# One broadcast transfer per block of x for both array halves, in a fused attention and bilinear-GLU kernel

## Chip, cores and metric

The kernel runs on one core of one Trainium2 chip. The metric is the device time of one launch in microseconds (us); the time before is the median of three runs.

## What is computed

x has 2048 tokens of width 576; attention has 32 heads of 18, and the GLU an inner width of 4608. Everything is float32.

```python
xn = layernorm(x)                                        # [1, 2048, 576], no scale or bias
q, k, v = heads(xn @ wqkv)                               # 32 heads of 18
s = concat(softmax(q @ k.T * 18 ** -0.5) @ v) @ wo
g = silu(((xn @ w_gate) * (xn @ w_up)) @ w_down)         # inner width 4608
out = x + s * g
```

## The kernel before

Float32 operands are split into a high and a low part, and each product is made of three matmuls (high by high, low by high, high by low), which is why x, the weights and the softmax inputs exist twice.

The kernel has a short first stage (layer norm, transposes of x into columns, the projections to q, k and v), one long main loop, and a short end (the projection with wo, silu, sum). In the main loop three kinds of work are interleaved on TensorE:

- scores: `a_item` (L651) makes scores for the row maxima, `b_item` (L703) makes them again for the exponentials;
- `pv_group` (L714): a visit, in which all of TensorE multiplies probabilities by v, 64 matmuls, about 7 us, twice per head;
- the GLU: `gu_op` (L756) for gate and up, `down_op` (L807) for the down projection.

Scores and GLU use 64 of the 128 rows of the array, so two streams run side by side on the two array halves. Half 0 (partitions 0 to 63) does the up products, half 1 (partitions 64 to 127) the gate products. Each half reads its own copy of x, from its own partitions.

The GLU goes over four chunks of 512 tokens (`NCH`); within a chunk over 18 units (`NF2`) of two column tiles each. The columns of x for the current chunk stand in the two tiles `xg` (`xc` in the profile), each 128 partitions x 9 slots x 512. They hold nine blocks of 64 input columns, each with a high and a low part; block b lies in slots 2b and 2b + 1, counted over both tiles, so that block 4 is cut between them. A tile of gate or up is 27 matmuls, three for each block in order (`TERMS`). There is one buffer for x: in the last tile of a chunk, each block of the next chunk is loaded over the one just used, from the copy `sx` in DRAM. That happens three times, at the three passages from one chunk to the next; the first chunk is loaded by `x_first` (L535).

Before the change each half brings its own copy as soon as it has itself used the blocks: half 0 by the queue of SyncE (SP), half 1 by that of GpSimd (Pool). Blocks 0 and 1, 2 and 3, 5 and 6, 7 and 8 come in pairs (L468), block 4 in two parts (L465), each to 64 partitions. On SP stand also the loads of weights (`wgu`, `wd`), of the q and k stacks (`whole`, `turning`, 18 rows each, L319) and of raw weights. Every queue is served in program order.

The order of the instructions is written out ahead by a planner (`order`). It keeps a clock for each half (`clk`), times at which the engines come free (`free`, `engine`) and one for the DMA queue (`moved`), takes the next instruction of the half that lags, and lets it go if `can_go` says that its inputs are due. For x that is `there["x", chunk, block, half]`, asked for the first tile of a new chunk only. TensorE then runs this order as it stands and waits on semaphores where a due time was too early.

```python
def moved(start, size):                                          # L1024
    queue[0] = max(queue[0], start) + size / 0.24
    return queue[0] + 2.0
...
if c and q == 0 and n % 2 == 0:                                  # L1216, in can_go
    return there.get(("x", c, k // 3, r), 1e9) <= now
```

When the gate tile is done, VectorE multiplies it with up (L769), ScalarE rounds the product to its high part (L774), and Pool makes the low part (L787).

Of the kernel before, what the change touches and what calls it, by code (L numbers as in the profile page):

```python
# [20 lines left out]
FT = mybir.dt.float32  # L21
# [20 lines left out]
def kernel(  # L42
# [10 lines left out]
    nc = tc.nc  # L53
# [20 lines left out]
    sx = dram.tile([NCH, 9, 64, 2, 512], FT, name="sx")  # L74
# [93 lines left out]
    clk, free, split_at = [0.0, 0.0], {"DVE": 0.0, "ACT": 0.0, "POOL": 0.0}, {}  # L168
# [7 lines left out]
    def engine(eng, start, length):  # L176
        start = max(free[eng], start)
        free[eng] = start + max(length - HIDDEN[eng], 0.03)
        return start + length
# [278 lines left out]
    def x_part(b, part):  # L458
        return divmod(2 * b + part, 9)

    def x_block(c, b, r):
        queue = nc.gpsimd if r else nc.sync
        if b == 4:
            for part in range(2):
                queue.dma_start(xg[part][r:r + 64, 8 - 8 * part, :].bitcast(FT), sx[c, b, :, part, :])  # L465
        elif b in (1, 3, 6, 8):
            i, k = x_part(b - 1, 0)
            queue.dma_start(xg[i][r:r + 64, k:k + 4, :].rearrange("p (b e) s -> p b e s", b=2).bitcast(FT),  # L468
                            sx[c, b - 1:b + 1].rearrange("b p e s -> p b e s"))

    vbox, vrows, vturn = {}, [], [0]

# [125 lines left out]
    for t in range(8, NT):  # L598
# [4 lines left out]
        if t == 11:  # L603
            xg = [xcp.tile([128, 9, 512], FR, name="xc")]
# [28 lines left out]
    with ExitStack() as mid:  # L633
# [115 lines left out]
        def gu_start(r, n):  # L749
            ready(gdone, n)  # L750
            return bank("g", 1, slots[r, "g"])

        def gu_op(r, n, ps, k):
            a, b, part = TERMS[k]
            i, e = x_part(b, part)
            nc.tensor.matmul(ps, gw[n][half[r], a, :], xg[i][half[r], e, :], start=k == 0,  # L756
                             stop=k == len(TERMS) - 1)
# [39 lines left out]
        def alone(u, n):  # L797
            return u == len(units) - 1 and n == 7

        def down_start(r, u):  # L800
            ready(ddone, u)
            return bank("g", 1, slots[r, "d"])

        def down_op(r, u, s, i, ps, n, by):
            own = alone(u, 2 * s + i)
            j, a, e = DTERMS[n]
            op = nc.tensor.matmul(ps[:, 0:HALF], hs[u][half[r], j, a, s * 128:(s + 1) * 128],  # L807
                             dw[u][half[r], j, e, i * HALF:(i + 1) * HALF],
                             start=(own or r == 0) and n == 0, stop=(own or r == 1) and n == len(DTERMS) - 1)
            if not own and r == 0 and n == len(DTERMS) - 1:  # L810
                handing[u, s, i] = by.nop()
                after(handing[u, s, i], op)
            if not own and r == 1 and n == 0:
                after(op, handing.pop((u, s, i)))
# [9 lines left out]
        def by_act(u, i, at):  # L824

            if units[u][1] == 0:
                return i == 1
            if u == len(units) - 1 or len(sums_later) == 2 or len(st_end) > 1 and st_end[-2 + len(sums_later)] > at:
                return False
            return max(free["ACT"], at) < max(free["DVE"], at)  # L830
# [18 lines left out]
        def down_end(u, s, i, ps, act):  # L849
            c, q = units[u]  # L850
            cs = slice(i * HALF, (i + 1) * HALF)
            if q == 0 and c >= 2:
                ready(sdone, 4 * c - 8 + s)
            a = sums(4 * c + s)[:, cs]
            if s == 3:
                seen[u] = seen.get(u, 0) + 1
                if seen[u] == 2:
                    d_get(u + 1)
            if act:
                if q == 0:  # L860
                    nc.scalar.activation(a, ps[:, 0:HALF], AF.Copy)
                else:
                    st = mp.tile([128, HALF], FT, name="st", bufs=2)
                    nc.scalar.activation(st, ps[:, 0:HALF], AF.Copy)  # L864
                    sums_later.append((a, st, u, s))
                    return
            elif q == 0:
                nc.vector.tensor_copy(a, ps[:, 0:HALF])
            else:
                nc.vector.tensor_tensor(a, a, ps[:, 0:HALF], op=OP.add)  # L870
            down_summed(u, s)
# [69 lines left out]
        def wo_fetch():  # L941
            wos[0] = xcp.tile([128, 8, D], FR, name="wos", tag="xc")
            for k in (0, 4):
                nc.sync.dma_start(wos[0][:, k:k + 4, :].bitcast(FT), swo[:, k:k + 4, :])
# [2 lines left out]
            wos[1] = wpool.tile([128, 2, D], FR, name="wos2", tag="wgu", bufs=2)  # L947
            nc.sync.dma_start(wos[1].bitcast(FT), swo[:, 8:10, :])

        passed, xdone = {}, []  # L950

        def stream(r, kind):

            def glu(n):
                c, q = units[n // 2]
                box = []
                for k in range(len(TERMS)):
                    def work(k=k):
                        if k == 0:
                            box.append(gu_start(r, n))  # L960
                        gu_op(r, n, box[0], k)
                        if q == NF2 - 1 and n % 2 and k % 3 == 2 and c < NCH - 1:
                            b = k // 3
                            x_block(c + 1, b, 64 * r)
                            if b in (1, 3, 4, 6, 8):
                                if r:
                                    at = engine("POOL", clk[r] + 0.5, 0.75 + 0.6 * (b == 4)) + 3.0
                                else:
                                    at = moved(clk[r] + 0.5, 0.285 if b == 4 else 0.57)
                                for e in (b,) if b == 4 else (b - 1, b):  # L970
                                    there["x", c + 1, e, r] = at
                        if n == 2 * len(units) - 1 and k == 13:
                            xdone.append(r)
                            if len(xdone) == 2:
                                wo_fetch()
                        if k == len(TERMS) - 1:
                            highs.append((gate_end if r else up_end)(n, box[0]))
                    end = (("DVE", 0.685) if r else ("ACT", 0.595)) if k == len(TERMS) - 1 else None
                    yield 0.231, k == 0, work, end, ("g", n, k), len(TERMS)

            def down(u, n):
                own = alone(u, n)
                key = u, n, r * own
                s, i = divmod(n, 2)
                for k in range(len(DTERMS)):
                    def work(k=k):
                        if (own or r == 0) and k == 0:
                            passed[key] = down_start(r, u)
                        down_op(r, u, s, i, passed[key], k, {"POOL": nc.gpsimd, "ACT": nc.scalar, "DVE": nc.vector}[soonest()])
                        if (own or r) and k == len(DTERMS) - 1:  # L990
                            acts.append(by_act(u, i, clk[r] + 0.33))
                            down_end(u, s, i, passed.pop(key), acts[-1])
                    end = None
                    if (own or r) and k == len(DTERMS) - 1:
                        end = (None, 0.0)
                    yield 0.132, (own or r == 0) and k == 0, work, end, ("d", u, 6 * n + k), len(DTERMS)

            if kind == "g":
                for n in range(2 * len(units)):
                    yield from glu(n)  # L1000
            else:
                for u in range(len(units)):
                    for n in range(8):
                        yield from down(u, n)
# [19 lines left out]
# [5 lines that stand above are left out]
        due, jobs, rows_done = [], [], {}  # L1029
        there, queue = {}, [0.0]  # L1030
        na = nb = 0
        part_work = len(units) * (2 * 27 * 0.231 + 4 * 12 * 0.132)
        part = part_work + (TOTAL + N + LEAD) * 0.231
# [199 lines left out]
        def soonest():  # L1233
            at = {eng: max(free[eng], clk[0] + 0.35 + (0.0 if eng == "POOL" else 0.2)) for eng in free}
            return min(at, key=at.get)
# [215 lines left out]
```

## Time and profile before

| | |
|---|---|
| median of three runs | 2621.14 us (2620.93 to 2621.47) |
| profiled execution, whole | 2619.56 us |
| its span, first to last instruction | 2617.8 us |
| TensorE, weight load, VectorE, ScalarE, GpSimd busy | 99%, 82%, 68%, 60%, 26% |
| mean granted TensorE clock | 0.998 |
| DMA: moved, mean rate | 434.33 MB, 166 GB/s |

Times are in us from the start of the span. Busy shares are of the span. In rows of the timeline stand the start, the duration, the engine (PE is TensorE, DVE VectorE, ACT ScalarE; SPq is SyncE's queue), the line, the operation, output and input tiles and count, and in brackets the idle time just before with what ended it. Rows of waits have the waiting instruction, what it waited for, then us in total, times, and the longest. Rows of windows give the stretch, the length, the busy time and count of TensorE, weight load, VectorE, ScalarE and GpSimd, the granted clock, the share of the 16 DMA engines that was busy (1 is all of them) and GB/s. Rows of DMA issues have the engine, the count, KB each, and for Pool the median us from issue to landing. A row with a spread of three numbers gives minimum, median and maximum in ns.

### The profile page before, as it was taken

The numbers are of one execution on the slowest core, as the hardware profiler recorded it, in microseconds if no ns is written. First come the engines' busy times: TensorE is split into PE (matmuls) and PEld (weight loads), VectorE is DVE, ScalarE is ACT, GpSimd is POOL, SyncE is SP. The second block draws the span as 40 slices with busy tenths as digits, with TensorE's granted clock in tenths as the row PEclk, the third lists the DMA queues.
The fourth block names the chain that finished last, engine by engine and source line by source line (L and its number), as shares of the span: only waits on it lengthen the run. The fifth ranks groups of instructions, "written<-read, shape, count | busy, mean of one in ns | idle before, by whom it ended". The sixth has DMA issues, their size and how long they took to land.

```text
span 2617.8 us, 59481 instructions
## 1 busy us (share of the span) xinstructions
PE 2595.7 (99%) x24504; PEld 2144.6 (82%) x24504; DVE 1782.2 (68%) x2951; ACT 1559.3 (60%) x3121; POOL 687.6 (26%) x721
## 2 busy tenths in 40 slices
PE   8999999999999999999999999999999999999999
PEld 7899878877778778878778887788888788877799
DVE  7208776767767777777767777677777777777136
ACT  4224666677766556666556666566666666666712
POOL 3114434444431212222121212222221222211015
PEclk9999999999999999999999999999999999999999
DMA  7799767676764445454564443453454443533366
GB/s 238 244 295 257 205 179 193 184 188 182 188 166 138 143 140 160 145 161 153 155 169 120 137 137 123 155 161 131 140 162 130 141 138 132 151 123 123 117 219 212
DMA packets 206544, 434.33 MB, mean 166 GB/s; under 512 B 82592, under 2 KB 132416, under 8 KB 176064
## 3 DMA queue, kind: packets, MB, share of 16 engines
q1 hardware_dynamic: 202096, 415.48, 52.5%
q0 software_dynamic: 4176, 15.04, 1.8%
q8 instruction: 193, 3.16, 0.5%
q14 instruction: 79, 0.65, 0.1%
HBM read 314.64 MB, written 110.56 MB: 162 GB/s over the span
## 4 chain that ended last, share of the span: by engine, by line
PE 96%; DMA 2%; SPq 1%; DVE 1%; issue 0%; ACT 0%; DVEq 0%
PE pg L756 35%; PE pg L714 17%; PE pg L807 16%; PE pa L651 11%; PE pb L703 9%; PE pg L1403 2%; PE pb L445 2%; PE pa L445 2%; PE pg L503 1%; DMA xc<-sx 1%; SPq L535 1%; DVE mx L653 0%; PE pb L1380 0%; DMA sv<-vo 0%; PE pa L703 0%; PE pg L385 0%
## 5 line engine op out<-in xcount | busy, mean ns | idle before, releaser
L653 DVE TENSOR_REDUCE mx<-pa 128x1 f32<-128x512 f32 x2016 | 1348.5, 687 | 379.1 <-PE pa L651 172.9
L705 ACT ACTIVATE pt<-pb 128x512 f32<-128x512 f32 x2003 | 1153.3, 603 | 501.1 <-PE pb L703 379.2
L756 PE MATMUL pg<-xc,wgu 64*128 64x512 f32 x7776 | 1401.9, 392 | 9.3 <-DMA xc<-sx 9.2
L756 PEld LDWEIGHTS pg<-xc,wgu 64*128 64x128 f32 x7776 | 1061.9, 186 | 55.6 <-DMA xc<-sx 6.4
L807 PE MATMUL pg<-wd,hs 64*128 64x288 f32 x6816 | 829.4, 293 | 0.0
L807 PEld LDWEIGHTS pg<-wd,hs 64*128 64x128 f32 x6816 | 775.9, 185 | 11.6 <-issue 1.7
L651 PE MATMUL pa<-whole,turning 54*128 54x512 f32 x1999 | 782.5, 398 | 0.8 <-DVE mx L653 0.7
L703 PE MATMUL pb<-whole,turning 56*128 56x512 f32 x1986 | 778.5, 398 | 0.0
L714 PE MATMUL pg<-pt,vt 128*32 128x512 f32 x4096 | 454.0, 595 | 0.0
L787 POOL TENSOR_TENSOR hs<-us,hs 128x512 fp32r<-128x512 f32 x144 | 185.9, 1291 | 1005.0 <-ACT hs L774 757.7
L651 PEld LDWEIGHTS pa<-whole,turning 54*128 54x128 f32 x1999 | 363.7, 184 | 71.5 <-issue 50.5
L703 PEld LDWEIGHTS pb<-whole,turning 56*128 56x128 f32 x1986 | 361.6, 184 | 7.7 <-ACT pt L705 0.6
L714 PEld LDWEIGHTS pg<-pt,vt 128*32 128x32 f32 x4096 | 126.6, 110 | 285.8 <-issue 281.5
L834 POOL TENSOR_TENSOR acc<-acc,st 128x288 f32<-128x288 f32 x290 | 233.3, 808 | 465.5 <-ACT st L864 297.1
L720 DVE TENSOR_TENSOR oc<-oc,pg 128x512 f32<-128x512 f32 x32 | 22.0, 688 | 220.5 <-PE pg L714 220.5
L254 POOL TENSOR_TENSOR wgu<-wraw,wgu 128x384 fp32r<-128x384 f32 x108 | 108.1, 1018 | 211.4 <-ACT wgu L253 120.0
L718 ACT ACTIVATE oc<-pg 128x512 f32<-128x512 f32 x32 | 19.1, 598 | 231.6 <-PE pg L714 231.6
L870 DVE TENSOR_TENSOR acc<-acc,pg 128x288 f32<-128x288 f32 x255 | 114.2, 449 | 41.4 <-PE pg L807 39.2
L769 DVE TENSOR_TENSOR us<-pg,us 128x512 f32<-128x512 f32 x144 | 98.5, 684 | 50.6 <-PE pg L756 31.6
L762 ACT ACTIVATE us<-pg 128x512 f32<-128x512 f32 x144 | 86.6, 602 | 69.2 <-PE pg L756 65.4
L864 ACT ACTIVATE st<-pg 128x288 f32<-128x288 f32 x290 | 119.9, 414 | 12.1 <-PE pg L807 6.0
L774 ACT ACTIVATE hs<-us 128x512 fp32r<-128x512 f32 x144 | 91.2, 634 | 26.1 <-DVE us L769 26.1
(147 smaller groups left out, 1288.7 us busy)
## 6 DMA issues: line engine op xcount, KB each, us to landing
wgu<-swg SPq DMA_DIRECT2D x102, 1152.0 KB
wd<-swd SPq DMA_DIRECT2D x50, 1152.0 KB
swg<-wgu SPq DMA_DIRECT2D x36, 1152.0 KB
whole<-sqk SPq DMA_DIRECT2D x192, 144.0 KB
turning<-sqk SPq DMA_DIRECT2D x384, 72.0 KB
swd<-wd SPq DMA_DIRECT2D x18, 1152.0 KB
sqk<-hl SPq DMA_DIRECT2D x32, 512.0 KB
wraw<-in_B_w_up_dram SPq DMA_DIRECT2D x36, 288.0 KB
```

The source lines that it names most:

```text
L254: nc.gpsimd.tensor_tensor(w[:, 9 + b:12 + b, :], raw[:, b:b + 3, :], w[:, b:b + 3, :].bitcast(FT), op=OP.subtract)
L651: nc.tensor.matmul(p, q[rows, t * 128:(t + 1) * 128], k[rows, c * 512:(c + 1) * 512], start=True, stop=True)
L653: nc.vector.tensor_reduce(mx[h][:, t, c:c + 1], p, axis=AX.X, op=OP.max)
L703: nc.tensor.matmul(p, k[rows, t * 128:(t + 1) * 128], q[rows, c * 512:(c + 1) * 512], start=True, stop=True)
L705: nc.scalar.activation(pt[t, c // 2][:, c % 2, :], p, AF.Exp, scale=scale)
L714: nc.tensor.matmul(p[32 * c:32 * c + 32, :], vt[h // 2][:, t, 6 * (h % 2):6 * (h % 2) + 32], pt[t, c // 2][:, c % 2, :], start=t == ts[0], ...
L756: nc.tensor.matmul(ps, gw[n][half[r], a, :], xg[i][half[r], e, :], start=k == 0, stop=k == len(TERMS) - 1)
L787: nc.gpsimd.tensor_tensor(hj[:, 1, :], h32, hj[:, 0, :].bitcast(FT), op=OP.subtract)
L807: op = nc.tensor.matmul(ps[:, 0:HALF], hs[u][half[r], j, a, s * 128:(s + 1) * 128], dw[u][half[r], j, e, i * HALF:(i + 1) * HALF], start=( ...
L834: nc.gpsimd.tensor_tensor(a, a, st, op=OP.add)
L864: nc.scalar.activation(st, ps[:, 0:HALF], AF.Copy)
L870: nc.vector.tensor_tensor(a, a, ps[:, 0:HALF], op=OP.add)
```

## The change

Each block comes by itself, in one transfer over all 128 partitions: the source is read twice, by a leading dimension of two with step 0. It is issued once both halves have used the block, by SP for even blocks and by Pool for odd ones; block 4 goes in two parts, one for each tile. In the planner each block counts 0.45 MB on the DMA queue, an odd one also 0.75 us on Pool and 2 us more, and both halves get the same due time.

```diff
-    def x_block(c, b, r):
-        queue = nc.gpsimd if r else nc.sync
+    def both_halves(tile, src):
+        return tile.bitcast(FT), src.unsqueeze(0).broadcast_to([2] + list(src.shape))
+
+    def x_block(c, b):
+        queue = nc.gpsimd if b % 2 else nc.sync
         if b == 4:
             for part in range(2):
-                queue.dma_start(xg[part][r:r + 64, 8 - 8 * part, :].bitcast(FT), sx[c, b, :, part, :])
-        elif b in (1, 3, 6, 8):
-            i, k = x_part(b - 1, 0)
-            queue.dma_start(xg[i][r:r + 64, k:k + 4, :].rearrange("p (b e) s -> p b e s", b=2).bitcast(FT),
-                            sx[c, b - 1:b + 1].rearrange("b p e s -> p b e s"))
+                queue.dma_start(*both_halves(xg[part][:, 8 - 8 * part, :], sx[c, b, :, part, :]))
+        else:
+            i, k = x_part(b, 0)
+            queue.dma_start(*both_halves(xg[i][:, k:k + 2, :], sx[c, b]))
...
-        passed, xdone = {}, []
+        passed, xdone, xhalf = {}, [], set()
...
                             b = k // 3
-                            x_block(c + 1, b, 64 * r)
-                            if b in (1, 3, 4, 6, 8):
-                                if r:
-                                    at = engine("POOL", clk[r] + 0.5, 0.75 + 0.6 * (b == 4)) + 3.0
-                                else:
-                                    at = moved(clk[r] + 0.5, 0.285 if b == 4 else 0.57)
-                                for e in (b,) if b == 4 else (b - 1, b):
-                                    there["x", c + 1, e, r] = at
+                            if (c, b) in xhalf:
+                                x_block(c + 1, b)
+                                at = moved(clk[r] + 0.5, 0.45)
+                                if b % 2:
+                                    at = max(at, engine("POOL", clk[r] + 0.5, 0.75) + 2.0)
+                                there["x", c + 1, b, 0] = there["x", c + 1, b, 1] = at
+                            xhalf.add((c, b))
```

## The prediction

> **What bounds the kernel now.** I read the page first (engines, slices, chain), then the table of waits, then the timeline around the three places where the change acts, then the DMA share in short windows.
>
> ```profile
> span 2617.8 us, 59481 instructions
> PE 2595.7 (99%) x24504; PEld 2144.6 (82%) x24504; DVE 1782.2 (68%) x2951; ACT 1559.3 (60%) x3121; POOL 687.6 (26%) x721
> PE 96%; DMA 2%; SPq 1%; DVE 1%; issue 0%; ACT 0%; DVEq 0%
> PE pg L756 <- DMA xc<-sx: 9.2, 3, 4.0
> PEld pg L756 <- DMA xc<-sx: 6.4, 2, 3.3
> ```
>
> TensorE is busy for 99% of the span and carries 96% of the chain. The kernel is bound by the order of its matmuls, and whatever makes TensorE stand still is paid in full. The loads of x touched here (xc<-sx) are the one DMA on which a main-loop matmul waits for long: 9.2 us in three waits. (The 6.4 us of PEld lie over the same stretches, so they are not added.) The waits stand in the timeline of TensorE:
>
> ```profile
> 754.01 1.05 PE L756 MATMUL pg<-xc,wgu 64*128 64x512 f32 x5 [3.96 <-DMA xc<-sx]
> 1360.73 0.50 PE L756 MATMUL pg<-xc,wgu 64*128 64x512 f32 x2 [2.89 <-DMA xc<-sx]
> 1365.66 0.79 PE L756 MATMUL pg<-xc,wgu 64*128 64x512 f32 x2 [2.37 <-DMA xc<-sx]
> ```
>
> They fall at the first two of the three passages from one chunk of 512 tokens to the next. The third passage has none. So what can be won is 9.2 us, 0.35% of the span. What can be lost depends on how long the new loads take.
>
> **What moves.** The issues of x, from the list of DMA issues, and the loads that stand near them in SP's queue:
>
> ```profile
> xc<-sx SPq DMA_DIRECT2D x12, 512.0 KB
> xc<-sx POOLq DMA_DIRECT2D x12, 512.0 KB, 13.7
> xc<-sx SPq DMA_DIRECT2D x6, 128.0 KB
> xc<-sx POOLq DMA_DIRECT2D x6, 128.0 KB, 13.5
> swd<-wd SPq DMA_DIRECT2D x18, 1152.0 KB
> draw<-in_B_w_down_dram SPq DMA_DIRECT2D x18, 576.0 KB
> whole<-sqk SPq DMA_DIRECT2D x192, 144.0 KB
> turning<-sqk SPq DMA_DIRECT2D x384, 72.0 KB
> ```
>
> Per passage, before: SP brings 4 x 512 + 2 x 128 = 2304 KB to half 0, Pool the same to half 1; together 4608 KB (4.72 MB). After: the same bytes, in other pieces. SP brings blocks 0, 2, 6, 8 (512 KB each, to both halves) and block 4 in two pieces of 256 KB, that is 2560 KB (2.62 MB); Pool brings blocks 1, 3, 5, 7, 2048 KB. SP issues six DMAs as before, Pool four instead of six.
>
> ```profile
> L468 SPq DMA_DIRECT2D xc<-sx x12: 599/610/656, 739.3 to 1934.4; - x12
> L468 POOL DMA_DIRECT2D xc<-sx x12: 592/597/746, 741.7 to 1936.0; - x12
> ```
>
> An issue costs about 0.6 us on either engine, so Pool saves some 1.1 us per passage. Pool is 26% busy and nobody waits for it there: nothing on the path. I take the issue cost as unchanged.
>
> **How a transfer is spread.** This is the step that decides. The windows show the share of the 16 DMA engines that were busy and what they moved, for three kinds of load:
>
> ```profile
> 1909.70 0.34 SPq L244 DMA_DIRECT2D wgu<-swg  x1
> 1910.09 1.06 SPq L319 DMA_DIRECT2D whole<-sqk  x3
> 1912.50:1913.50 1.00, 1.00 (x17) 1.00 (x15) 0.94 (x2) 1.00 (x4) 1.00 (x2) 1.00 1.04 442
> 1914.60:1916.60 2.00, 2.00 (x30) 2.00 (x28) 1.89 (x5) 1.99 (x5) 1.26 (x2) 1.00 0.58 143
> 1349.00:1357.00 8.00, 8.00 (x91) 7.97 (x90) 6.49 (x12) 4.77 (x9) 1.61 (x2) 1.00 1.04 278
> 1936.00:1946.00 10.00, 10.00 (x104) 4.98 (x98) 4.66 (x9) 3.03 (x6) 1.85 (x2) 1.00 1.05 280
> ```
>
> In the first window the weights wgu (128 rows of the tile) are under way: share 1.04, all 16 engines, 442 / (1.04 x 16) = 26.6 GB/s each. In the second only the three `whole` loads behind them are left, each of 18 rows: share 0.58, which is 9 of 16 (0.56), although SP has nothing else to send; 143 / (0.58 x 16) = 15.4 GB/s each. The two windows on x (64 rows, both queues) have all engines busy at 278 / (1.04 x 16) = 16.7 GB/s each. So a transfer does not always get 16 engines. 9 is the largest number up to 16 that divides 18, and 16 divides 64 and 128: the split goes over the leading count of the transfer. In the new one the destination's leading count is 128, but the source's is 2: `unsqueeze(0).broadcast_to([2, ...])` puts the two copies first, with step 0, which cannot be merged with the 64 rows behind it. A split that has to cut both sides into the same number of parts finds 2. I take it that each new transfer runs on two DMA engines, one for each half. No row of before shows a transfer with a leading count of 2, so this is inferred from 18, 64 and 128.
>
> The Trainium skill ("DMA: Bandwidth & Descriptors", Rules for kernel authors) speaks against the change in the same direction: a leading zero-stride broadcast of c copies keeps the whole DMA on at most c engines. By that rule the sum is the one below; no run so far shows it.
>
> **The sum.** Successive SP transfers would use the same two engines, since a later one waits behind the earlier. Each carries half of SP's 2.62 MB, 1.31 MB. At 26.6 GB/s that is 49 us, at 16.7 78 us, at 15.4 85 us. The slow rows are those in which the transfers fill 18 or 64 rows of the tile, the fast one fills 128, as the new ones do; so I take a value near the fast end, 55 us (24 GB/s, for pieces of 4 KB where wgu's are 9 KB), and keep 49 and 85 for the range. Before, the same passage needs 4.72 MB / 0.278 = 17 us.
>
> When do they start, and when are they needed? A block is now fetched once the later half has used it. Half 1 is the later one; its first pair was issued here, after six of its matmuls:
>
> ```profile
> 741.72 0.75 POOL L468 DMA_DIRECT2D xc<-sx  x1 [0.88 <-PE pg L756]
> 1338.86 0.61 POOL L468 DMA_DIRECT2D xc<-sx  x1
> 1930.04 0.61 POOL L468 DMA_DIRECT2D xc<-sx  x1 [9.20 <-PE pa L651]
> 779.26 0.68 DVE L769 TENSOR_TENSOR us<-pg,us 128x512 f32<-128x512 f32 x1
> 1369.15 0.69 DVE L769 TENSOR_TENSOR us<-pg,us 128x512 f32<-128x512 f32 x1 [1.50 <-PE pg L756]
> 1961.93 0.68 DVE L769 TENSOR_TENSOR us<-pg,us 128x512 f32<-128x512 f32 x1
> ```
>
> Block 0 needs three matmuls fewer, 0.7 us at the kernel's own 0.231 each: 741.0, 1338.2, 1929.3. The L769 rows are the product that closes the first tile of the new chunk, about 1.3 us (three matmuls and the passage to VectorE, my estimate) after its block 8 can start. From issue to use I add the 2.0 us that the kernel's planner has (L1027). On the two engines lies also their part of what else SP sends there: at the first passage a sixteenth of swd and draw and a ninth of three `whole` (108 + 48 KB, 6.0 us at 26.6 GB/s), at the second three `whole` (1.8 us), at the third three `turning` (0.9 us).
>
> - First: 741.0 + 2 + 55 + 6.0 + 1.3 = 805.3, against 779.3: 26.0 us later.
> - Second: 1338.2 + 2 + 55 + 1.8 + 1.3 = 1398.3, against 1369.2: 29.1 us.
> - Third: 1929.3 + 2 + 55 + 0.9 + 1.3 = 1988.5, against 1961.9: 26.6 us.
>
> Together 81.7 us, in which the old 9.2 us of waits are already replaced. TensorE takes its instructions in the written order, so while it waits for x no other tile, score or visit fills in; all of it is on the path. After the waits of before the granted clock is down:
>
> ```profile
> 1365.00:1367.00 2.00, 1.33 (x6) 1.14 (x8) 0.04 (x1) 0.08 (x1) 0.00 (x0) 0.50 0.51 185
> 1367.00:1369.00 2.00, 2.00 (x13) 1.05 (x15) 0.65 (x1) 0.52 (x1) 0.00 (x0) 0.50 0.30 124
> ```
>
> These 4 us at 0.50 do the work of 2, so the reduced clock costs 2 us or a little more per passage. The first two passages pay that already; at the third it will be new, taken as 3. Sum: 84.7 us.
>
> What is queued behind the added wait: SP now waits for the later half too.
>
> ```profile
> 739.34 0.63 SPq L468 DMA_DIRECT2D xc<-sx  x1
> 1336.14 0.66 SPq L468 DMA_DIRECT2D xc<-sx  x1
> 1927.87 0.64 SPq L468 DMA_DIRECT2D xc<-sx  x1
> DMA to landing us min/median/max: 9.0/13.7/20.3
> ```
>
> Against the first Pool rows above that is 2.2 to 2.7 us later, for x and for the stack loads (`turning`, `whole`) and weights behind it, and on the two engines these stand behind x. They come in while TensorE waits for block 8 and are hidden by that wait; without it they would cost up to 2.7 us per passage. (The last row is Pool's transfers of x before, from issue to landing.) Pool's four transfers take 512 KB on two engines each, 0.26 MB per engine, 10 us at 26.6 GB/s, and if they get other engines than SP's they are done long before. The planner's due times for x change too (0.45 MB of its queue per block against 0.57 per pair on SP alone, 16.9 us against 10.7 us for all nine at 0.24 MB/us). The last block is then due about 2 + 17 us after its start, at 760, 1357 and 1948, ahead of when it was used before; so I cost the reordering at nothing, with 10 us either way.
>
> The profiled execution took 2619.56 us (1.8 us around the span), the median of three 2621.14 us. 2621.1 + 84.7 = 2705.8, so 2706.
>
> **Rivals.** 1. *The split follows the 128 destination rows* and each transfer gets 16 engines. Then 4.72 MB go at up to 442 GB/s in 11 us instead of 17, the start is some 2 us later on SP, and the 9.2 us of waits vanish: 2621 - 9 = 2612, 2616 if the later start shows. For it speaks that wgu's 128 rows run so; against it the 9 engines of `whole`, whose shape, like this one, is not a multiple of 16 in front. It decides from the point where the last block lands under 30 us after the first issue. The Trainium skill (same page and section) also advises one 128-partition transfer in place of two to disjoint halves, which would lead here; the trace has both halves at 278 GB/s against 442. Chance 0.10.
> 2. *Spread over 16, but what the faster transfer wins the later start takes*: 2618 to 2625, no change. Chance 0.04.
> 3. *Pool's transfers fall on SP's two engines.* Then all 4.72 MB go over two engines, 2.36 MB each, 89 us at 26.6 GB/s, and each passage takes 34 us more than forecast: 2706 + 102 = 2808. The queue rows show nothing on which engines Pool's transfers take; a share of them would lie between. Chance 0.06.
>
> **The numbers.** The forecast, two engines per transfer, has 0.80. Its own ends: at 49 us per passage 18 us less, 10 us for the order, and some more if the tail is covered: 2665. At 78 to 85 us, 69 to 90 us more: up to 2790. That range holds 8 in 10; rivals 1, 2 and most of 3 are left outside. A measurement of this kernel can tell about 0.2%, 5 us. Faster by more: 0.10 (rival 1). Within: 0.04. Slower: 0.86.
>
> **What would show it.** In windows over the 50 us after 741, 1338 and 1929 the DMA share is well under 1, some 0.15 to 0.6, falling to 0.12 (two of 16) once Pool's are done. The wait of L756 for xc<-sx grows from 9.2 to some 80 to 90 us, in several steps at each passage, one per even block, 10 us apart; the third passage has them too. Pool's 512 KB land in 12 to 16 us. The work of the engines in the rest of the span is unchanged. Wrong: a share of 1 in those windows and waits under 10 us (rival 1 or 2), or last blocks landing 90 us after the first (rival 3). If the time grows without waits for x, the order is to blame and not the spread.

## The result and the profile after

| | before | after |
|---|---|---|
| median of five runs | 2620.93 us (2619.45 to 2621.47) | 2735.17 us (2734.01 to 2737.61) |
| span of the profiled execution | 2617.8 us | 2733.9 us |

The changed kernel takes 1.0438 times as long (95% interval 1.0423 to 1.0454), 114 us more; 2706 us were forecast, with 2665 to 2790 as the range. Lines in the rows of the changed kernel are two higher than before (L758 is the gate and up matmul, L771 the product). From its page (span, busy time of each engine, granted clock by slices, and the chain of waits by engine):

```profile
span 2733.9 us, 59474 instructions
PE 2624.1 (96%) x24504; PEld 2146.5 (79%) x24504; DVE 1780.3 (65%) x2947; ACT 1559.6 (57%) x3125; POOL 690.4 (25%) x719
PEclk9999999999979999999989999999988999999999
PE 89%; DMA 8%; DVE 1%; SPq 1%; ACT 0%; issue 0%; ACTq 0%; DVEq 0%
```

From its table of waits (sum in us, count, longest):

```profile
PE pg L758 <- DMA xc<-sx: 92.1, 17, 15.2
PE pb L705 <- DMA whole<-mr: 4.3, 1, 4.3
```

The span grew by 116.1 us. TensorE stood still for 2733.9 - 2624.1 = 109.8 us, where it was 22.1 before: 87.7 us more, of which the waits for x are 92.1 - 9.2 = 82.9. The other 28.4 us are busy time: the same 24504 matmuls took 2624.1 instead of 2595.7 us. They ran slower because the granted clock fell: the row of slices has a 7 and three 8s, at the three passages, and the windows below show 0.50 there. VectorE and ScalarE are as before.

Windows of 5 us in the three passages (two for each; length, busy time of PE, PEld, DVE, ACT and POOL with their instructions, and at the end granted clock, DMA share and GB/s) show what the loads did:

```profile
770.00:775.00 5.00, 5.00 (x50) 1.38 (x41) 0.10 (x1) 0.00 (x0) 0.00 (x0) 1.00 0.14 54
805.00:810.00 5.00, 4.25 (x30) 4.11 (x32) 2.06 (x3) 2.42 (x5) 0.73 (x1) 0.62 0.13 52
1405.00:1410.00 5.00, 2.70 (x12) 1.90 (x14) 0.00 (x1) 0.40 (x1) 0.00 (x0) 0.50 0.13 48
1435.00:1440.00 5.00, 0.00 (x0) 0.00 (x0) 0.00 (x0) 0.00 (x0) 0.00 (x0) 0.68 0.13 52
2035.00:2040.00 5.00, 1.52 (x7) 1.04 (x7) 0.00 (x0) 0.60 (x1) 0.00 (x0) 0.50 0.13 51
2055.00:2060.00 5.00, 0.40 (x2) 0.00 (x0) 0.00 (x0) 0.00 (x0) 0.00 (x0) 0.50 0.13 52
```

A share of 0.13 is two engines of 16, at 52 / 2 = 26 GB/s each. In five of the six windows TensorE is idle for a part or at a lowered clock; in the first it runs a visit, which needs no x. Before, the same columns read 1.04 and 278.

How long each passage is can be read from the products that close the last tile of a chunk and the first tile of the next. Three rows of before (the others stand in the prediction), then the six of after:

```profile
747.76 0.69 DVE L769 TENSOR_TENSOR us<-pg,us 128x512 f32<-128x512 f32 x1 [0.21 <-PE pg L807]
1345.13 0.69 DVE L769 TENSOR_TENSOR us<-pg,us 128x512 f32<-128x512 f32 x1
1935.89 0.68 DVE L769 TENSOR_TENSOR us<-pg,us 128x512 f32<-128x512 f32 x1
```

```profile
747.97 0.69 DVE L771 TENSOR_TENSOR us<-pg,us 128x512 f32<-128x512 f32 x1 [0.28 <-PE pg L809]
820.97 0.69 DVE L771 TENSOR_TENSOR us<-pg,us 128x512 f32<-128x512 f32 x1 [0.18 <-PE pg L758]
1388.30 0.68 DVE L771 TENSOR_TENSOR us<-pg,us 128x512 f32<-128x512 f32 x1
1445.28 0.68 DVE L771 TENSOR_TENSOR us<-pg,us 128x512 f32<-128x512 f32 x1
2014.24 0.68 DVE L771 TENSOR_TENSOR us<-pg,us 128x512 f32<-128x512 f32 x1
2086.19 0.68 DVE L771 TENSOR_TENSOR us<-pg,us 128x512 f32<-128x512 f32 x1
```

The passages took 31.5, 24.0 and 26.0 us; now they take 73.0, 57.0 and 72.0. That is 41.5, 33.0 and 45.9 us more, 120.4 together, of which some 4 us are regained elsewhere. All of the loss is at the three passages. The order moved work as well: over the second passage TensorE ran 182 matmuls before and 252 now (259 and 263 at the first, 267 and 253 at the third). Why the second is shorter than the others is one of the questions below.

### The profile page after: what moved, and what is told of

Read it like the earlier page. It is cut to its first block, busy times and chain, and to the rows that moved or that the text cites. A ratio compares the mean times of both kernels' runs of the same rounds, so it can differ in the third digit from the quotient of the medians.

```text
span 2733.9 us, 59474 instructions
## 1 busy us (share of the span) xinstructions
PE 2624.1 (96%) x24504; PEld 2146.5 (79%) x24504; DVE 1780.3 (65%) x2947; ACT 1559.6 (57%) x3125; POOL 690.4 (25%) x719
## 3 DMA queue, kind: packets, MB, share of 16 engines
q0 software_dynamic: 14640, 14.30, 1.6%
## 4 chain that ended last, share of the span: by engine, by line
PE 89%; DMA 8%; DVE 1%; SPq 1%; ACT 0%; issue 0%; ACTq 0%; DVEq 0%
PE pg L758 33%; PE pg L716 16%; PE pg L809 15%; PE pa L653 10%; PE pb L705 8%; DMA xc<-sx 6%; PE pg L1404 2%; PE pb L445 2%; PE pa L445 1%; PE pg L505 1%; DMA whole<-mr 1%; SPq L537 1%; DMA sqk<-hl 0%; SPq L319 0%; DVE mx L655 0%; DMA draw<-in_B_w_down_dram 0%
## 5 line engine op out<-in xcount | busy, mean ns | idle before, releaser
L758 PE MATMUL pg<-xc,wgu 64*128 64x512 f32 x7776 | 1430.4, 396 | 92.2 <-DMA xc<-sx 92.1
L758 PEld LDWEIGHTS pg<-xc,wgu 64*128 64x128 f32 x7776 | 1066.0, 188 | 159.2 <-DMA xc<-sx 79.8
L809 PE MATMUL pg<-wd,hs 64*128 64x288 f32 x6816 | 845.6, 295 | 0.0
L809 PEld LDWEIGHTS pg<-wd,hs 64*128 64x128 f32 x6816 | 787.0, 187 | 11.5 <-issue 0.8
L771 DVE TENSOR_TENSOR us<-pg,us 128x512 f32<-128x512 f32 x144 | 98.5, 684 | 60.3 <-PE pg L758 36.4
```

## The experiments

All are the changed kernel with one thing altered, unless the text says otherwise. Theory A is that of the prediction: the number of DMA engines that a transfer gets is the largest up to 16 that divides the leading count of both sides, here two.

**Two transfers of 64 rows for each block.** Same order, due times, queues and waits; only the spread differs.

```diff
-            queue.dma_start(*both_halves(xg[i][:, k:k + 2, :], sx[c, b]))
+            for r in (0, 64):
+                queue.dma_start(xg[i][r:r + 64, k:k + 2, :].bitcast(FT), sx[c, b])
```

(and likewise for block 4)

> The changed kernel with the same order of matmuls, the same due times, the same wait for both halves and the same queue for each block, but each broadcast transfer cut in two plain ones of 64 rows. Theory A (the leading two of the source puts each transfer on two DMA engines): the loads run on 16 engines again, the 172 us of waits for x fall to under 15 us, the DMA share at the passages is near 1, and the time is 2612 to 2626 us. Theory B (single blocks, the wait for the later half and the new order cost the time): it stays at 2700 us or more.

Measured: 2612.21 us (2610.66 to 2613.15), 0.997 of the kernel before (0.9959 to 0.9982). Its span, from its page; then its waits for x, a window in the first passage, and the landings of Pool's transfers, each from its own view:

```profile
span 2610.2 us, 59526 instructions
```

```profile
PE pg L760 <- DMA xc<-sx: 0.2, 1, 0.2
```

```profile
745.00:755.00 10.00, 10.00 (x102) 6.63 (x102) 5.83 (x10) 4.52 (x9) 4.29 (x7) 1.00 1.00 308
```

```profile
DMA to landing us min/median/max: 5.7/10.9/15.1
```

All engines are busy, at 308 GB/s, and the waits for x are gone. Theory B falls: with the same order, due times and wait for the later half the loss is gone; the form of the transfer costs 123 us. This version is faster than both kernels, by 0.3% than the kernel before.

**A source of 128 plain rows.** The copy in DRAM holds every block twice.

```diff
-    sx = dram.tile([NCH, 9, 64, 2, 512], FT, name="sx")
+    sx = dram.tile([NCH, 9, 2, 64, 2, 512], FT, name="sx")
...
-            queue.dma_start(*both_halves(xg[i][:, k:k + 2, :], sx[c, b]))
+            queue.dma_start(*both_halves(xg[i][:, k:k + 2, :], sx[c, b].rearrange("h p e s -> (h p) e s")))
```

(`both_halves` returns its source as it is; `x_store` writes each block twice)

> The changed kernel, but the copy of x in DRAM holds both copies of every block, so that each transfer has 128 plain rows as its source; same queues, same order in the main loop. The first stage writes x twice. Theory A: 16 engines per transfer, 4.72 MB in 11 to 17 us per passage, waits for x under 10 us; 2612 to 2626 us, plus 0 to 20 us for the 7 MB more that the first stage writes. A rival theory, that transfers over all 128 partitions are slow in themselves: 2700 us or more.

Measured: 2642.27 us, 1.0085 (1.0072 to 1.0099). That is inside the range of theory A with its 0 to 20 us for the first stage, but the parts are not as expected. Rows of the first visit, from the timeline of the kernel before and of this one, with this one's span ahead and Pool's landings behind:

```profile
289.78 1.49 PE L714 MATMUL pg<-pt,vt 128*32 128x512 f32 x12
```

```profile
span 2641.8 us, 59550 instructions
```

```profile
324.59 1.92 PE L719 MATMUL pg<-pt,vt 128*32 128x512 f32 x16
```

```profile
DMA to landing us min/median/max: 6.0/7.9/11.1
```

The first visit starts 34.8 us later, the end comes 24.0 us later: the first stage, in which only the writes of x were changed, costs more than the expected 0 to 20 us, and from the first visit on 10.8 us are won. No matmul waits for x. Transfers over all 128 partitions are therefore not slow in themselves; Pool's land in 7.9 us.

**Rows of 62 and 2, without a repeated source.** The two-by-64 kernel, each transfer cut again.

```diff
             for r in (0, 64):
-                queue.dma_start(xg[i][r:r + 64, k:k + 2, :].bitcast(FT), sx[c, b])
+                for p0, p1 in ((0, 62), (62, 64)):
+                    queue.dma_start(xg[i][r + p0:r + p1, k:k + 2, :].bitcast(FT), sx[c, b, p0:p1])
```

> The two-by-64 kernel with each plain transfer of 64 rows cut into one of 62 and one of 2 rows; no source is repeated. Theory A (the split goes over the largest number up to 16 that divides the leading count: 2 for 62 and for 2): SP's 2.62 MB per passage are on two engines again, without any zero step, the DMA share at the passages falls to 0.13 as in the changed kernel, and the time is 2690 to 2745 us. Theory F (it is the repeated source, the step of zero, that makes a transfer slow): the loads run as with 64 rows, 2610 to 2630 us with the issues doubled.

Measured: 2731.17 us, 1.0422 (1.0406 to 1.0438). Windows in the first and third passage:

```profile
770.00:775.00 5.00, 0.60 (x6) 0.17 (x3) 1.24 (x3) 1.19 (x2) 0.00 (x0) 0.84 0.13 52
2035.00:2040.00 5.00, 1.70 (x6) 1.05 (x6) 0.05 (x1) 0.00 (x0) 0.00 (x0) 0.64 0.13 50
```

With plain transfers and 62 rows in front the picture is that of the changed kernel: share 0.13, 52 GB/s. So the zero step is not what slows a transfer (theory F falls); a leading count of 2 is, and so is one of 62, whose largest divisor up to 16 is also 2. The Trainium skill ("DMA: Bandwidth & Descriptors", Why a DMA increments its semaphore by 16 and not by 1) states just this rule: the largest number up to 16 that divides the slowest dimension of both sides. The trace agrees for 2 in the changed kernel, for 62 here, and for 18 (share 0.58) before, on SP's queue. Pool's transfers of 62 rows went over more than two. The trace has every DMA packet with its start and length: at the first passage more than ten of Pool's data packets are under way at once for 3.1 us, in the changed kernel for less than 0.1, and the transfers landed after 8.7 us (median) where those took 34.1. What is said here of 62 rows is therefore shown for SP alone.

**All transfers by SP, all by Pool.**

```diff
-        queue = nc.gpsimd if b % 2 else nc.sync
+        queue = nc.sync         # in the other kernel: nc.gpsimd
```

> The changed kernel with all ten broadcast transfers of a passage issued by SP, same order of matmuls. Theory A: 4.72 MB over SP's two engines, 2.36 MB each, 89 to 95 us per passage where SP's 2.62 MB took 59 to 75, so 20 to 35 us more per passage: 2795 to 2840 us, at a DMA share of 0.13 for most of it. Theory B (order and the wait for both halves): as the changed kernel, 2735 us.

> The changed kernel with all ten broadcast transfers of a passage issued by Pool, same order of matmuls. Theory A with SP's transfers always on the same two engines and Pool's on changing ones: a passage's ten transfers spread over all engines, 10 to 20 us each side by side, so the last block lands some 30 us after the first issue and the time is 2620 to 2660 us. Theory C (each transfer has two engines, and all of them, Pool's too, the same two): 4.72 MB over two engines take 90 us, and the time is 2800 us or more.

SP alone: 2826.53 us (one run), as theory A has it. Its waits for x, and a window of the first passage:

```profile
PE pg L758 <- DMA xc<-sx: 167.9, 25, 9.2
```

```profile
810.00:815.00 5.00, 2.87 (x14) 2.32 (x16) 0.83 (x2) 1.59 (x3) 0.70 (x1) 0.50 0.13 52
```

4.72 MB instead of 2.62 MB over SP's two engines cost 91 us more than the changed kernel. Pool alone: 2673.02 us, 1.0207 (1.0193 to 1.0221). Theory C falls, since Pool's transfers do not share one pair; but the time lies above the 2620 to 2660 us expected. Its waits show why:

```profile
POOL xc L471 <- DMA xc<-sx: 59.1, 5, 25.4
PE pg L758 <- DMA xc<-sx: 26.1, 1, 26.1
PE pg L809 <- POOLq L813: 32.6, 2, 16.3
```

Pool was held for 59.1 us by its own transfers: in each passage it issued eight of the ten at once and the last two only after earlier ones had landed. At the first passage that reached TensorE as a wait for x, at the others through Pool's queue: L813 is the step by which a bank is handed from one array half to the other, and it stood on Pool behind the held transfers. 26.1 + 32.6 = 58.7 us; the median is 53 us above that of the kernel before.

**One pair further in Pool's rotation.**

```diff
+    turn_on = accp.tile([128, 8], FT, name="turn_on")
+    nc.gpsimd.dma_start(turn_on, x2[0:64, 0:8].unsqueeze(0).broadcast_to([2, 64, 8]))
```

> The changed kernel plus one tiny broadcast transfer by Pool before the main loop (64 rows of 32 bytes, to both halves of a tile that nobody reads). Theory A2 (Pool's transfers take pairs of engines in rotation, eight engines per passage, so that at the first and third passage one of the four falls on SP's pair and slows SP's by 10 us, and at the second none): the rotation is shifted by one pair, the first and third passage become free of it, about 10 us shorter each, and the second about 10 us longer, 2720 to 2730 us in all. If Pool's transfers do not rotate: no change, 2735 us.

Measured: 2729.2 us (2727.13 to 2730.26), 1.0413 (1.0398 to 1.0427). The same six rows of the closing products:

```profile
748.96 0.69 DVE L773 TENSOR_TENSOR us<-pg,us 128x512 f32<-128x512 f32 x1 [0.29 <-PE pg L811]
813.66 0.69 DVE L773 TENSOR_TENSOR us<-pg,us 128x512 f32<-128x512 f32 x1 [0.19 <-PE pg L760]
1381.27 0.68 DVE L773 TENSOR_TENSOR us<-pg,us 128x512 f32<-128x512 f32 x1
1448.08 0.68 DVE L773 TENSOR_TENSOR us<-pg,us 128x512 f32<-128x512 f32 x1
2017.45 0.68 DVE L773 TENSOR_TENSOR us<-pg,us 128x512 f32<-128x512 f32 x1
2078.68 0.68 DVE L773 TENSOR_TENSOR us<-pg,us 128x512 f32<-128x512 f32 x1
```

The passages take 64.7, 66.8 and 61.2 us in place of 73.0, 57.0 and 72.0: 8.3 less, 9.8 more, 10.7 less. A transfer of no use to anyone, issued some 550 us before the first passage, moved some 10 us from two passages to one. This is what theory A2 expects: Pool's transfers take pairs in rotation, four pairs per passage, and one of the four falls on SP's pair either at the first and third passage or at the second. This is a small part of rival 3 of the prediction.

**Where the 8 us of the two-by-64 kernel come from.** Three kernels. First, the kernel before with other due times only:

```diff
-                                if r:
-                                    at = engine("POOL", clk[r] + 0.5, 0.75 + 0.6 * (b == 4)) + 3.0
-                                else:
-                                    at = moved(clk[r] + 0.5, 0.285 if b == 4 else 0.57)
+                                at = moved(clk[r] + 0.5, 0.225 if b == 4 else 0.45)
+                                if r:
+                                    at = max(at, engine("POOL", clk[r] + 0.5, 0.75 + 0.6 * (b == 4)) + 3.0)
```

> The kernel before, with its own transfers (64 rows, pairs of blocks, each half by itself), and only the planner's due times for x changed: 0.45 MB of the DMA queue for each pair and half (0.225 for a part of block 4's half), 4.05 MB per passage in all, as the changed kernel counts it. Theory D (what the two-by-64 kernel gained over the kernel before comes from the later due times, which put other work where TensorE waited 9.2 us): waits for x under 3 us, 2610 to 2616 us. Theory E (it comes from single blocks, which land sooner): as before, 2617 to 2624 us.

Measured: 2619.47 us, 0.9998 (0.9989 to 1.0007), no change, so theory D falls. 4.0 us of waits for x are left in place of 9.2; what was won there came back as waits for a stack (1.6 us) and for weights (1.2), and as 3.7 us more of busy time. Second, the kernel before with single blocks:

```diff
-        elif b in (1, 3, 6, 8):
-            i, k = x_part(b - 1, 0)
...
+        else:
+            i, k = x_part(b, 0)
+            queue.dma_start(xg[i][r:r + 64, k:k + 2, :].bitcast(FT), sx[c, b])
```

(with due times of 0.225 MB for each)

> The kernel before with its own queues (SP for half 0, Pool for half 1) and each half fetching as soon as it has itself used a block, but block by block in place of pairs, with due times of 0.225 MB per block and half. Theory E (single blocks land sooner and each matmul then waits for less): waits for x under 3 us and 2610 to 2616 us, as the two-by-64 kernel. Theory G (what helps is that both halves' copies of a block come one after the other, so that neither half has to wait for the slower queue): 2617 to 2623 us, with waits of 4 us or more left.

Measured: 2623.77 us, 1.0019 (1.0009 to 1.0028), slower by 0.2%. Its waits:

```profile
POOL xc L468 <- DMA xc<-sx: 9.1, 3, 4.1
PE pg L806 <- POOLq L810: 4.9, 2, 3.8
PE pa L650 <- DMA turning<-sqk: 3.7, 1, 3.7
```

Theory E falls too, and theory G only half holds: no matmul waits for x any longer, but ten transfers per passage on Pool hold Pool itself, and 4.9 us come back through the handing step, 3.7 us through a stack load. Third, the two-by-64 kernel with the smaller due cost:

```diff
-                                at = moved(clk[r] + 0.5, 0.45)
+                                at = moved(clk[r] + 0.5, 0.285)
```

> The two-by-64 kernel with the planner counting 0.285 MB of the DMA queue per block in place of 0.45, 2.57 MB per passage as the kernel before did. If the truthful due times are what keeps TensorE from waiting: some 3 to 9 us of waits for x come back and 2614 to 2621 us. If the blocks land early enough anyway: 2610 to 2614 us.

Measured: 2611.44 us, 0.9969 (0.9958 to 0.9981), as with 0.45. So the due times are not the reason either. The gain itself is in the waits: TensorE stands still for 14.2 us in the two-by-64 kernel (2610.2 - 2596.0) and for 22.1 before. What the two faster kernels have and the two others lack is that both halves' copies of a block go out together, with the blocks divided between SP and Pool (eight transfers on Pool, twelve on SP). That the gain comes from this is likely but not shown: the order of the matmuls differs between these kernels too, and that alone can be worth some microseconds.

## Why the prediction was right, and where it was off

**The spread over two engines, the step that decided, was right.** Share 0.13 at 52 GB/s after, the 62-row kernel with the same picture, and the 64- and 128-row kernels without it show the cause. Rivals 1 and 2 are ruled out. What rival 1 would give if it held, no waits for x, was measured too with the two transfers of 64 rows: 2612 us, as it said. Against the forecast the passages took 15.5, 3.9 and 19.3 us more; the paragraphs below say in which terms. (In the range, 90 us more on 2706 are 2796 and not 2790; nothing hangs on it.)

**The rate was taken slightly low.** 24 GB/s per engine were assumed, between 15.4 and 26.6; 26 were measured. The row with 128 rows was the right neighbour. By the rate alone a passage would have been some 4 us shorter than forecast.

**The time from first issue until block 8 can be used** was forecast as 63.0, 58.8 and 57.9 us. From the timeline, SP's first issue and TensorE's last wait for x at each passage, and the visit that follows the third (start, length, engine, line; the wait stands in brackets); then a window of this visit:

```profile
740.64 0.61 SPq L471 DMA_DIRECT2D xc<-sx  x1
815.78 0.79 PE L758 MATMUL pg<-xc,wgu 64*128 64x512 f32 x1 [5.00 <-DMA xc<-sx]
1380.23 0.57 SPq L471 DMA_DIRECT2D xc<-sx  x1
1440.29 0.79 PE L758 MATMUL pg<-xc,wgu 64*128 64x512 f32 x2 [7.29 <-DMA xc<-sx]
2006.11 0.57 SPq L471 DMA_DIRECT2D xc<-sx  x1
2064.92 1.22 PE L758 MATMUL pg<-xc,wgu 64*128 64x512 f32 x4 [9.52 <-DMA xc<-sx]
2067.35 7.52 PE L716 MATMUL pg<-pt,vt 128*32 128x512 f32 x64
```

```profile
2069.00:2075.00 6.00, 6.00 (x57) 1.65 (x49) 0.00 (x1) 0.00 (x0) 0.00 (x0) 1.00 0.13 52
```

At the first two passages the last wait is for block 8, and the time was 75.1 and 60.1 us. At the third the last wait, 58.8 us after the first issue, is for block 6: x still comes at share 0.13 during the visit, and by the packet records of SP's queue block 8 was complete at about 2076, some 70 us after the first issue. So the second agrees with the forecast, and the first and third are 12 us longer. Most of that is one of Pool's transfers on SP's pair, 8.3 and 10.7 us by the rotation kernel. The prediction had Pool's transfers on other engines than SP's and left a share of them on the same to rival 3; one in four at two of the passages is what the runs show. Where the rest of the 12 us went was not followed.

**The step that failed is the time from block 8's landing to the closing product**, taken as 1.3 us everywhere. At the first and second passages it was 5.2 and 5.0 us, at the third about 10 (2086.2 - 2076). There the 4.3 us wait for `whole<-mr` came after block 8, up to 2079.6, and then matmuls at half clock (0.50 from 2080 to 2085). The prediction had the stack loads behind x come in while TensorE waits for block 8, hidden by that wait; at the third passage block 8 landed during a visit, and this load after it. I had costed the reordering at nothing because the new due times lay ahead of the old use; the order shifted all the same, as the counts of matmuls above show.

**The lowered clock was undersized**: 3 us were added. The matmuls took 28.4 us longer in all. A part of them ran while the next block was still under way, where at full clock TensorE would only have waited longer for it; the runs don't say how large a part.

**The issue was not unchanged.** It was taken as 0.6 us. SP's timeline at the first passage:

```profile
743.57 3.06 SPq L471 DMA_DIRECT2D xc<-sx  x1
746.73 26.04 SPq L468 DMA_DIRECT2D xc<-sx  x2
772.82 13.08 SPq L319 DMA_DIRECT2D turning<-sqk  x3
```

Two issues of block 4 held SP for 26 us, the stack loads behind them for another 13. These loads were not merely behind x on the two engines, as I had it, but not even issued. That this alone cost time was not tested apart.

## What to carry to other kernels

Before a load is reshaped, look at the first dimension of both sides as it is written. In these runs SP's transfers got as many DMA engines as the largest number up to 16 that divides both: 2 for a broadcast written with its two copies in front, 2 for 62 rows, 9 for 18, 16 for 64 and 128. Two plain transfers of 64 rows did the job of the broadcast in 123 us less. A window with a flat, low DMA share and few GB/s, beside a consumer that waits, is how such a transfer looks in a profile. Look also at what stands behind it in the same queue, and at when that is needed.

## What the runs showed of the hardware that was not expected

- SP's issue of a transfer is not always short. L468 on SP took 3.7 us at least and 22.3 at most (`SPq DMA_DIRECT2D xc<-sx x6: 3687/10470/22257` ns), where 0.55 was usual before and 0.58 is the median with two transfers of 64 rows. It fits that SP is held while its two engines are behind; this was not tested apart.
- Pool's transfers of 512 KB landed after 34.1 us (median), not 12 to 16 as forecast, though 256 KB per engine take 10 us at 26 GB/s. The page's queue rows show that Pool's queue moved 14640 packets for 14.30 MB, where it was 4176 for 15.04 MB:

```profile
q0 software_dynamic: 14640, 14.30, 1.6%
```

  From the view of Pool's transfers, and the same queue in the stretch from 775 to 800 us:

```profile
DMA to landing us min/median/max: 16.5/34.1/46.3
```

```profile
q0 software_dynamic: 330, 0.00, 0.8%
```

  By the packet records of the first passage, Pool's four transfers made 512 packets of 4096 bytes, the last at 770.9 us, and 3648 packets of 4 bytes, the last at 793.2. So the data was there well before the last landing, and only small packets came after it. The kernels with plain transfers on Pool have 3888 to 4848 packets on this queue in all. That the small ones are late because they stand behind SP's backlog is an inference; it was not tested.
- One dummy transfer of Pool moved some 10 us between passages, so how Pool's transfers and SP's meet depends on how many such transfers went before.
